# An induced-attention and gated-MLP kernel: weighted sums in column groups, full-height scores, gates and tables, and a re-searched order

## The chip, the cores and the metric

The kernel runs on one NeuronCore of a Trainium2 chip. The metric is the device time of one execution in microseconds (us); lower is better. Engines are named as in the profile: PE is TensorE (matmuls; PEld are its weight loads), ACT ScalarE, DVE VectorE, POOL GpSimd, SP SyncE, which here only starts DMAs. PSUM, where matmuls put their results, has eight banks.

## The reference

Four batches of 12,416 tokens with 128 channels, 32 inducing vectors, and an MLP with 1536 hidden units:

```python
def mab(q, kv):
    s = scale * (q @ kv.transpose(0, 2, 1))
    s = s - s.max(-1, keepdims=True)
    a = np.exp(s)
    a /= a.sum(-1, keepdims=True) + 1e-09
    return a @ kv
h = mab(I, x)                       # I: (B, 32, 128), x: (B, 12416, 128)
attn = mab(x, h)
gate = np.maximum(attn @ w_gate, 0.0)
val = attn @ w_val
out = gate * val @ w_out            # (49664, 128) float32
```

## The kernel before, in words

The kernel never forms the hidden units of a token. A token's attention output is a mix of the 32 rows of h with positive weights p. If a hidden unit's gate has one sign for all mixes, gate times value is a quadratic form in p, and the output is a sum over pairs (m, n) of p_m p_n times a table row that depends on h and the weights alone. So a batch needs these steps (b is the batch; the names in brackets are the planner's):

- **Load and transpose.** A batch has 97 tiles of 128 tokens: six groups of 16, and one tile over. They come in on POOL's queue (line 296). Each group is transposed, on PE in halves of 64 rows (turn, line 640) with a copy by DVE (line 650), or by a DMA on SP's queue (line 658) for the groups in BY_DMA.
- **First scores (s1a, s1b; line 685).** For each token the 32 scores against the inducing vectors, two groups at a time into two banks. A matmul contracts over 64 of the 128 channels, on the low or the high half of PE's rows; a low and a high one run side by side, on different banks. Then the halves change banks, which is a second step behind a wait for the first (the helper two). ACT takes the exponential (line 699).
- **h and its weights (ha, hb; lines 718 and 729).** The exponentials are moved through x as the stationary operand, again in halves of 64 tokens, into two banks: 32 matmuls for a group's h, and 8 with one moving column for the sums. DVE adds them up over the three pairs of groups (hacc, lines 743 and 745). A short chain on DVE and PE (lines 755 to 794) divides by the sums and gives hT, with one more column for the sum over the inducing vectors.
- **Gates (g1, g2; line 884) and products.** hT times the weights w_gate and w_val, in halves and two steps; DVE makes masks and scaled copies, and 16 products U of shifted copies (line 989), and a fifth, narrower set, u58.
- **Tables (T, line 1033; T5, line 1068).** The products are contracted with w_out in halves of 64 rows, four tables T of 128 rows each, two at a time in two banks, each in two steps, and T5. DVE copies them out (lines 1050, 1052, 1082).
- **Second scores (S, line 819).** hT as a stationary operand of 32 columns, four column groups of PE at once with four tiles of tokens; DVE copies them out (line 831).
- **Pairs (e, line 1257; f, line 1266).** A matmul with a 0/1 matrix adds up two scores for each pair, and ACT takes the exponential of 1024 columns at a time, into a ring of six buffers F: 192 times in all, 48 per batch. e5 and F5 (lines 846 and 859) do it for the fifth table; er, or and os for the tile over.
- **Outputs (o, line 1312).** For each token tile, 18 half-height matmuls of F with the tables, in two steps a and b with a wait between. DVE normalises three tile pairs at once (lines 1339 and 1344) and SP stores them (line 1356).
- **Check.** POOL and DVE test that the signs hold (lines 1117 to 1172); if a count is left at the end, a general kernel follows. It is not run here.

The first batch's loads, transposes, first scores and h have a section of their own (lines 305 to 512), which ends about 28 us into the span; its matmuls are full height. Everything behind it is a list of steps that the class Plan puts in an order. Each step has an engine, a duration, the steps it depends on, and perhaps PSUM banks that it takes or frees. Within an engine the order is written out: ORDER holds, in two digits each, the numbers of the steps of PE, ACT, DVE, POOL and SP, and BANKS a bank for a step where there is a choice. Plan.order (lines 158 to 215) goes through these queues with the durations, and by the times that it reckons it interleaves the engines' instructions into one program. So the orders within the engines were found beforehand by a search over this model, and the durations decide which bank a step gets.

Of the kernel before, what the change touches and what calls it, by code (L numbers as in the profile page):

```python
# [20 lines left out]
NU = 3  # L21
# [4 lines left out]
BEGIN = {}  # L26
BY_DMA = {(2, 3), (3, 3), (2, 1), (3, 1), (2, 5), (3, 5)}
# [4 lines left out]
        "0600041T022f5b1j1B5e0c1n0d2j5h2h5u2L5v5k081h5n2N5A5B5x1V5q5y1R1P5D5E0z5G2t5H0A0B0C2z0D0E0F"  # L32
        "0G5s1z5J2P5K0Z1x0+0Q0R1l2v0S0T5O0U0V0W1D0X2R5U1p2d1q1r1s1t1F1u1G1H1I1J3m1K2l2x2m2n2o2p2B2q"
        "2C2D3i2E2F3k2G1X1Y1Z4c1+1-232024254g2627283S3g5Y0ab339b83A2-3w30313Q32332T342U2V3y2W2X3U2Y"
        "3b1c3C3c4Q5W5+bp644s65bq3E3F4O3G3H3I4w3Jbjbkbd3o3O3p3q4M3r3s423t4344bh45464u47bmbvbn7bbw3W"
        "bsbt4y3X3Y4K3Zby3+bz4i3-4S7f4T4U4e4V4W4+4X7p4-507N51527L4A534B4C7d4D4E8J4F6r6s6t6u8D8H6v6w"
        "6x6ybD608l4k6R4l4m6S4n4o7J4p6I7H6J6K6L896MbN6N797v6O6PbL7tbJ857h8b7i7j7rgU7k7lbR7m7P8p7Q7R"
        "877S7T7x7U7y7z9c7A7B7C917X9e7Y7Z8Fh27+9o7-80628d9u8e8fgZ8r8g8h8i9s74he938n94hfbVbPbW9M8th8"
        "8uh98v988w8x8y8L9a8M8N9G8O8P9qhbhcaq8Q8Tam8U8V9K8W8X9waI8Y9x9yh69z9Ahk9I9g9Bhl9h9iaa9j9k9O"
        "9l9P9Qa89R9SaG9Thhhia4a6hnho9Wd09X9Yak9Zac9+ao9-adaedCafagbTahcgchaEcicjd4ckasdAataueSavaw"  # L40
        "aCaxcldycmcndYhsaKd2aLaMd+aNaOaSdgaPaTaUdwaVaWewaXcGdWcHdkcxcyczdicAeuhycBdecCcDcEeehAdEey"
        "dFdGegdHdIdMdJc+dNdOeadPdQe0d6dRd7d8fvd9dafzdbdme-dndodpecdqe2drfhe3e4ese5e6fjeie7ejekf-el"
        "emf3eIeneJffeKeZeLeMcVf1hEeNfdhKfVhLeAfBeBfxeCeDg9eEeFflgrfmfngtfofpgxfqeUhGeVf5gbf6f7fXf8"
        "f9fDfagdfEfFfZfGfHgffLfIfMfNiTfOfPiPfQghiVgigjgkgvglg1gmjpg2g3j9g4g5jri5i6g6jni7i8j7i9iajL"
        "ibicivj3iwiRhCgzjlgAgBjNgCgDgHgEhIgIgJkcgKgLkaiminj5ioipk6iqirisk8itj-gMiXjRiYiZkqi+i-jbj0"
        "kujcjdkUjejfjPjtjgjujvkSjwjxksjBjyjCjDkojEjFkQkwjGl4kxkylokzkAkekBl6kfkglqkhkijTkjl2jUjVl8"
        "jWjXlkkEjYkFkGkOkHkIlmkJiKm2k1k2lAmqlBlClOlDlElalFlbm4lcmoldlekWlfkXkYmkkZk+mmlsk-ltlul+lv"
        "lwm0mwlxmxmylKmzmAlQmgmBmhlMmimjmsmtlSlTlUlVlWm6lXm7m8m9mambmH"
    ),
    (  # L50
        "1U2g1k1C1o2k2i2M5w091i2O5C1W1S1Q2u5I2A5t1A2Q1y1m2w1E2e2S2y3n3j3l4d4h3T3h0b3a3B3x3R3z3V3D4R"
        "4tbr4P4xbl3P4Nbi4v7cbx4z4L4j7g4f7q7O7M7e8K8I8E8m617K7I8a7a7w7u868c7sbS8q889d929f8G9p639v8s"
        "9t8ohg9Nha999b9H9raran9LaJh79Jhmaba9aHa5a7d1alapdDbUaFd5dBeTaDdzdZd3d-dhdxexdXdldjevdfefez"
        "ehc-ebe1fwfAf0edfietfkg0f4fge+f2fefWfCfygagsgugyhHgcfYgef+ggiUiQiWgwjqjajsjoj8jMj4iSjmjOhJ"
        "kdkbj6k7k9k0jSkrkvkVjQkTktkpkRl5lpl7lrl3l9llkPlnm3mrlPm5mpmlmnl-m1lLlRlN"
    ),
    (
        "070105035c5f0e0g0k0f5i0i0h0j0m0l5l0w0s0n0p5o0v0x0t0r5z5r0y0K0u0J0o5F0I0q0L0O0H0M5L0N5M0P0-"
        "5N1e1f5P5Q5R5S5T0Y5V1v1w1L1M2r2s2H2I2122292a5Zb4b91a1b35362Z2+3d3e1d5-5X686667696a6c6b3K6d"
        "3L6jbe6B3u3v766f48496ebo6k6lbu6n6p6q6CbAbB40416m6D4Y4Z6h6o5477556g4G6i4HbC6A6z6HbE6F6EbF6G"  # L60
        "6TbG4q4rbHbIbO6QbMbKgV7n7o7V7W7D7E72h3818273g+8j8k759596bQbXbZb+b-bYc1c0c28z8Ac3c4hd8R8Scp"
        "c6ca8Z8+9C9Dc8cX9m9nce9Uc9hj9Vcrcbhpcfcca0a1cscdaic5ajcYc7cqhqhrayazcohtcuctcwcvaQaRhuaYaZ"
        "cIhvhwhxhzcFhBdKdLdSdTdcddcTdsdte8e9cUeoepcWhFeOePhPhOhMhNhQhShRhTi1eGeHhZfrfshUeWeXi3igif"
        "fbfchVhXfJfKi4fRfSh-i2gngoi0h+hWg7g8hYihidilixiehDikiigFgGijiugNgOj1j2jhjijzjAjHjIiMkCkDkk"
        "kliIjZiJj+kKkLk3iLk4lGlHlglhiNl0l1lylzmCmDmumGmvlYlZmcmdmI"
    ),
    (
        "b55a5d5g5j5m5p58b0b2bagWbfgYgRgT10b7bcg-1112131415161718191gh1h46U6V6W6X6Y6Z6+6-707178cJcK"
        "cLcMcNcOcPcQcRcScZiyiziAiBiCiDiEiFiGiHiO"
    ),  # L70
    (
        "59bb1N1O2J2c2b2Kbgb6b137383f3M3N4b4a57564I4Jh5h0gX7G7F8384gS978C8B908-9E9Fa2a3aAaBa+a-dVdU"
        "dudvereqeQeReYftfUfufTgqgpgPgQjjjkjKjJkmknkNkMk5liljlJlImEmFmemfmJ"
# [7 lines left out]
    "2-2-1-0-----1---------------------------------------2-----------------------0------------1"  # L81
    "---------------------------------1-------2-----------------1------------------------------"
    "---2-------1-----------2------------0---------------2-----------------0-------2-----------"
    "----------------------0-----------------1-------1------------2-----0--1--1--1------0-----1"
    "-----2----1-----0---2-0----------------------------0----------------2--------0------------"
    "--0------------2---------------------------------0-------------------------2--------------"
    "-2-----------------0-------0--------------------------------------------------------------"
    "----0---------------------------------1--------------------------------------1------------"
    "------0-----------0----1-----1-2-0-1-----0----------------------1----------------2--------"
    "2--------------0------------0-----------------------------------------------------------2-"  # L90
    "--------------0-----------------2-------------------0------------2---------------2--------"
    "---------2-------0-----------------0---------------1-----------------0-------0------------"
    "1----2----1--------0-----------2----------1---0-1-----0----------------------2------------"
    "-------------0--------------0------------1---------------------------------2-------1------"
    "----------------------------------1-----------------0-------0-----------------0-----------"
    "----0-------------------------------------------1-------------------------1---------------"
    "1----------2--"
# [4 lines left out]
class Op:  # L102
    __slots__ = (
        "name", "eng", "dur", "post", "deps", "emit", "take", "frees", "goal", "dma", "near",
# [4 lines left out]
class Plan:  # L109
# [3 lines left out]
    BANKS = {"E": 2, "D": 4}  # L113
    ENGINES = ("PE", "ACT", "DVE", "POOL", "SP")

# [3 lines left out]
    def op(self, name, eng, dur, emit, deps=(), post=None, take=None, frees=(), goal=1e9, dma=0.0):  # L119
        o = Op()  # L120
        o.name, o.eng, o.dur, o.emit, o.take, o.goal, o.dma = name, eng, dur, emit, take, goal, dma
        o.post = {"PE": 0.21, "ACT": 0.15, "DVE": 0.07, "POOL": 0.1, "SP": 0.1}[eng] if post is None else post
        o.frees = [f for f in frees if f]
# [34 lines left out]
    def order(self, begin, sequences, near=()):  # L158
# [12 lines left out]
        done = []  # L171
        while len(done) < len(ops):
            best = None
            for e in self.ENGINES:
# [50 lines left out]
def quadratic_body(ctx, tc, x, inducing, moe_w_gate, moe_w_val, moe_w_out, out):  # L225
# [39 lines left out]
    ones16 = keep([P, P], FP16, "ones16")  # L265
    indT = keep([P, M], FP16, "indT")
# [38 lines left out]
    def first_batch(sp, psum):  # L305
# [33 lines left out]
        dve.memset(ones16, 1.0)  # L339
        warm = st([P, BLK], FP16, "warm", 1)  # L340
# [262 lines left out]
    def two(step, n, mm, o, prev):  # L603

        if step:
            after(*prev.tail)
        for i in range(n):
            ya = mm(0, step, i)
            yb = mm(1, 1 - step, i)
        o.tail = (ya, yb)  # L610
        return o.tail

# [3 lines left out]
    def prepare(b):  # L616
        s = state[b]
        s["turn"], s["load"] = {}, {}
        for q in (NQ, *range(NQ)):
# [13 lines left out]
            if q < NQ and (b, q) not in BY_DMA:  # L633
                o = op(f"turn{b}.{q}", "PE", 0.55, None, [load, *(war or [])], take=("D", 2))
# [20 lines left out]
            else:  # L655
# [10 lines left out]
        o = op(f"s1r{b}", "PE", 0.25, None, [s["turn"][NQ]], take=("E", 1))  # L666
# [4 lines left out]
                out=p1r[:, 0:M], in_=ebanks(o)[:, 0, 0:M], func=AF.Exp, scale=sm_scale  # L671
# [991 lines left out]
```

## Time and profile before

| | |
|---|---|
| median of 3 runs | 299.63 us (299.54 to 303.91) |
| profiled execution | 300.5 us, of which 298.5 us span |
| instructions in the span | 15,634 |
| PE busy, granted clock (mean) | 255.7 us, 0.94 |
| ACT busy | 215.0 us |
| DVE busy | 186.8 us |
| first matmul behind the first batch's section | 28.72 us |
| first output matmul (line 1312) | 72.04 us |
| last output matmul issued, end of the span | about 289, 298.5 us |

The profile is a page for one execution with busy times by engine, forty slices of the span, DMA queues, and groups of instructions; the trace behind it can be asked for the waits of an engine (who waited for whom), for instructions in order of time, and for busy times and counts of instructions in any stretch. A releaser "issue" means that the engine waited for nothing that the profile shows. Times of matmuls include the pipeline behind them, so the price of a matmul in a row of equal ones is read from the difference of start times, not from its length.

### The profile page before, as it was taken

What the parts mean: (1) busy time and instruction counts of PE and PEld (TensorE: products, weight loads), DVE (VectorE), ACT (ScalarE), POOL (GpSimd) and SP (SyncE); (2) the same over time, 40 slices, a digit from 0 to 9 for tenths busy, and PEclk for the clock granted to TensorE, in tenths of its full rate; (3) what the DMA queues carried; (4) which work ended last, traced back from release to release, by engine and by line L of the source; (5) the groups of instructions that cost most, each with busy time, mean ns of one, the idle gap of its engine ahead of it and who ended that gap; (6) DMA issues with size and microseconds to landing.
All of it is one profiled execution on the core that took longest, in us unless ns stands there. A gap on an engine that the chain in (4) does not pass through costs nothing.

```text
span 298.5 us, 15634 instructions
## 1 busy us (share of the span) xinstructions
PE 255.7 (86%) x7251; PEld 201.6 (68%) x7251; DVE 186.8 (63%) x383; ACT 215.0 (72%) x248; POOL 84.6 (28%) x146
## 2 busy tenths in 40 slices
PE   7497776787889784999998987999999999999970
PEld 3386444775666673885876775876877878887850
DVE  3656967366567672787576473785578794565560
ACT  4173757355479653879898875998999999999910
POOL 3594200149600310019502000079030004921200
PEclk9689976589999997999999997999999999999996
DMA  7989996659949736228950440341352250355343
GB/s 279 417 227 200 215 212 123 109 99 202 188 196 179 193 118 134 110 111 151 171 210 21 172 155 2 120 168 40 125 199 113 96 231 4 127 196 224 136 185 116
DMA packets 30039, 46.83 MB, mean 157 GB/s; under 512 B 16624, under 2 KB 17296, under 8 KB 29968
## 3 DMA queue, kind: packets, MB, share of 16 engines
q1 hardware_dynamic: 25056, 35.04, 35.6%
q0 software_dynamic: 4864, 10.72, 19.8%
q8 instruction: 58, 0.95, 1.4%
q14 instruction: 13, 0.11, 0.1%
q10 hardware_dynamic: 48, 0.02, 0.0%
HBM read 27.80 MB, written 25.43 MB: 178 GB/s over the span
## 4 chain that ended last, share of the span: by engine, by line


## 5 line engine op out<-in xcount | busy, mean ns | idle before, releaser
L1266 ACT ACTIVATE F<-AL 128x1024 f16<-128x1024 f32 x192 | 184.1, 1030 | 45.2 <-PE AL L1257 43.8
L1312 PE MATMUL AL<-T,F 64*128 64x129 f16 x3456 | 134.7, 219 | 5.4 <-issue 3.6
L1312 PEld LDWEIGHTS <-F 64*128 64x128 f16 x3456 | 108.0, 95 | 32.5 <-PE AL L1312 18.6
L1257 PE MATMUL AL<-S,pairs 64*128 64x512 f16 x384 | 75.0, 387 | 2.0 <-ACT F L1266 1.2
L1344 DVE TENSOR_TENSOR osb<-AL,rzo 128x768 f32<-128x768 f32 x64 | 61.2, 956 | 2.7 <-DMA out_dram<-osb 0.8
L1117 POOL TENSOR_TENSOR far<-S 128x768 f16<-128x768 f16 x16 | 23.4, 1467 | 84.4 <-DVE U L989 83.8
L1339 DVE RECIPROCAL rzo<-AL 128x6 f32<-128x6 f32 x64 | 12.5, 196 | 47.7 <-PE AL L1312 47.1
L1033 PE MATMUL AL<-wo,U 64*128 64x128 f16 x768 | 29.1, 227 | 1.0 <-issue 1.0
L1033 PEld LDWEIGHTS <-U 64*128 64x128 f16 x768 | 25.3, 100 | 5.1 <-issue 2.0
L1257 PEld LDWEIGHTS <-pairs 64*128 64x128 f16 x384 | 22.1, 95 | 6.1 <-issue 4.7
L1117 POOL TENSOR_TENSOR far<-far 128x768 f16<-128x768 f16 (+2 forms) x20 | 25.0, 1249 | 1.6
L296 POOL DMA_DIRECT2D x<-in_x_dram x18 | 9.7, 553 | 40.1 <-PE AL L729 19.0
L650 DVE COPY xT<-AL 128x2048 f16<-128x2048 f16 x12 | 14.6, 1220 | 6.3 <-PE AL L640 6.1
L831 DVE CAST S<-AL 128x1024 f16<-128x1024 f32 x12 | 14.3, 1214 | 2.6 <-PE AL L819 2.5
L1157 POOL TENSOR_SCALAR eps<-eps 128x1 f32<-128x1 f32 x4 | 0.8, 189 | 49.2 <-DVE eps L1142 49.2
L718 PE MATMUL AL<-p,x 64*128 64x32 f16 x576 | 10.8, 176 | 3.9 <-issue 3.8
L685 PE MATMUL AL<-indT,xT 64*128 64x32 f16 x576 | 10.8, 175 | 3.6 <-DMA xT<-x 1.4
L685 PEld LDWEIGHTS <-xT 64*128 64x128 f16 x576 | 9.7, 94 | 5.5 <-issue 3.0
L718 PEld LDWEIGHTS <-x 64*128 64x128 f16 x576 | 9.9, 95 | 5.3 <-issue 4.7
L427 DVE COPY xT<-xT_ps 128x1024 f16<-128x1024 f16 (+1 forms) x15 | 8.5, 582 | 6.8 <-PE xT_ps L426 6.7
L447 ACT ACTIVATE p1a<-s_ps 128x256 f16<-128x256 f32 (+2 forms) x16 | 5.2, 332 | 10.1 <-PE s_ps L445 9.9
L699 ACT ACTIVATE p<-AL 128x1024 f16<-128x1024 f32 x9 | 9.2, 1021 | 3.2 <-PE AL L685 3.2
(157 smaller groups left out, 270.9 us busy)
## 6 DMA issues: line engine op xcount, KB each, us to landing
out_dram<-osb SPq DMA_DIRECT2D x64, 384.0 KB, 3.3
x<-in_x_dram POOLq DMA_DIRECT2D x18, 512.0 KB, 11.2
x<-in_x_dram SPq DMA_DIRECT2D x9, 512.0 KB, 6.5
x<-in_x_dram SPq DMA_DIRECT2D x6, 256.0 KB, 7.9
wg<-in_moe_w_gate_dram POOLq DMA_DIRECT2D x1, 384.0 KB, 4.8
wv<-in_moe_w_val_dram POOLq DMA_DIRECT2D x1, 384.0 KB, 7.1
wo<-in_moe_w_out_dram POOLq DMA_DIRECT2D x1, 384.0 KB, 8.4
out_dram<-osr SPq DMA_DIRECT2D x4, 64.0 KB, 2.3
```

Source lines behind the costliest of these rows:

```text
L296: pool.dma_start(out=x16(b, t0, n), in_=xv[b][:, t0 : t0 + n, :])
L650: dve.tensor_copy(out=xTs[q].rearrange("p t (h j) -> p h t j", h=2), in_=ps)
L685: return pe.matmul(ps[:, k, t, :], xTs[qs[k]][ROWS[half], t, :], indT[ROWS[half], :], start=step == 0 and t == 0, stop=step == 1, skip_gro ...
L718: pe.matmul(ps[:, r, 0:M], l, m, start=k == 0 and t == 0, stop=k == 1, skip_group_check=True,)
L831: dve.tensor_copy(out=S[b % 2][:, gs[0] : gs[0] + 2, :], in_=dbanks(o))
L1033: pe.matmul(ps[:, k, 0:P], U[js[k] % NU][r, i, t].rearrange("p k m -> p (k m)"), wo[r, t, :], start=(step, i, t) == (0, 0, 0), stop=(step, ...
L1117: pool.tensor_tensor(out=dst, in0=in0, in1=in1, op=f)
L1257: pe.matmul(ebanks(o)[:, r, :], pairs[ROWS[r], par, j, :], S[b % 2][ROWS[r], g, :], start=True, stop=True,)
L1266: lambda o=o, j=j: act.activation(out=dst[:, j], in_=ebanks(o), func=AF.Exp, scale=sm_scale,),
L1312: pe.matmul(ps[:, k_, :], l, m_, start=step == 0 and j == 0, stop=step == 1 and j == n - 1,)
L1339: lambda: dve.reciprocal(out=rzo[rr], in_=view()[:, :, :, P : P + 1]),
L1344: lambda: dve.tensor_tensor(out=dst[:, :, 3 * h6 : 3 * h6 + 3, :], in0=view()[:, :, :, 0:P], in1=rzo[rr].broadcast_to([P, 2, 3, P]), op=AL ...
```

## The change

Four things change together.

- First scores, gates, tables and T5 use all 128 rows in one matmul, and no second step. The helper two goes. A table takes one bank instead of two tables taking two, with its own copy.
- h and its weights: the exponentials become the stationary operand of 32 columns, and x moves (128 columns), spread over four column groups of PE by tile number; the sums are made likewise with a matrix of 1/32 (part16). One step ha replaces ha and hb; hacc is now 256 columns wide, and the sums over the four groups are made by a matmul with stackI (the step zp, which has two products now).
- The model of the search gets two terms: SWITCH, 0.1 for a change of tiling (each step has a mode: 0 for halves, 1 for full height, 2 for column groups), and Fetch, which counts PE's instructions (rec) and delays PE where a block of 256 is worked off before the next is there. Some PE durations are changed with it (S 0.65 to 0.44, turn 0.55 to 0.50, vp 0.6 to 0.4).
- ORDER and BANKS are new throughout, so the orders of all five engines are.

```diff
+FETCH = (100, 256, 3.5, 1.0)
 ORDER = (
...
 class Plan:
+    SWITCH = 0.1
+    class Fetch:
+        def __init__(self):
+            self.left, self.ahead = FETCH[0], 0.0
+        def late(self, o, server):
+            done, wait = 0, 0.0
+            while o.rec - done >= self.left:
+                done += self.left
+                t = o.start + wait + o.dur * done / o.rec
+                wait += max(0.0, self.ahead - t)
+                t = max(t, self.ahead)
+                self.ahead = t + FETCH[2] + (FETCH[3] if server > t else 0.0)
+                self.left = FETCH[1]
+            self.left -= o.rec - done
+            return wait
...
+                if e == "PE" and o.mode != mode:
+                    t += self.SWITCH
...
+            if o.eng == "PE":
+                mode = o.mode
+                o.end += fetch.late(o, server)
...
+        dve.memset(part16, 1.0 / M)
...
-    p1r = main([P, P], FP16, "p1r")
-    pool.memset(p1r, 0.0)
+    p1r = main([P, M], FP16, "p1r")
-    hacc = main([P, 2, M + 1], FP32, "hacc")
+    hacc = main([P, 2 * P], FP32, "hacc")
...
-                def mm(k, half, t):
-                    return pe.matmul(
-                        ps[:, k, t, :], xTs[qs[k]][ROWS[half], t, :], indT[ROWS[half], :],
-                        start=step == 0 and t == 0, stop=step == 1, skip_group_check=True,
-                    )
-                two(step, CT, mm, o, o1)
+                    for t in range(CT):
+                        pe.matmul(ps[:, i, t, :], xTs[q][:, t, :], indT, start=True, stop=True)
...
-            ha = op(f"ha{b}.{u}", "PE", 0.52, None, [e], take=("D", 2))
-            hb = op(f"hb{b}.{u}", "PE", 0.52, None, [ha, s["p1r"] if rest else None])
+            o = op(
+                f"ha{b}.{u}", "PE", 0.57, None, [e, s["p1r"] if rest else None], take=("D", 1),
+                mode=2, rec=80 + 4 * rest,
+            )
+            def rows(o=o, b=b, qs=qs, dst=dst, rest=rest):
+                ps = dbank(o)
+                n = 2 * CT
+                flat = dst.rearrange("p k t m -> p (k t) m")
+                for t in range(n + rest):
+                    r = t % 4
+                    l = flat[:, t, :] if t < n else p1r
+                    x_ = x16(b, qs[t // CT] * CT + t % CT if t < n else NT - 1)[:, 0, :]
+                    pe.matmul(
+                        ps[32 * r : 32 * r + 32, 0:P], l, x_, start=t < 4,
+                        stop=t >= n - 4 + (rest and r == 0),
+                    )
+                for i in range(2):
+                    for r in range(4):
+                        t = 8 * r + 4 * i
+                        pe.matmul(
+                            ps[32 * r : 32 * r + 32, P : 2 * P], part16,
+                            flat[:, t : t + 4, :].rearrange("p t m -> p (t m)"),
+                            start=i == 0, stop=i == 1 and not (rest and r == 0),
+                        )
...
+            pe.matmul(dbank(o)[:, 0:M], hacc[:, 0:P], stackI[:, 0, :], start=True, stop=True)
+            pe.matmul(dbank(o)[:, M : 2 * M], ones32, small["zs"], start=True, stop=True)
...
+            for k, w in enumerate((wg, wv)):
+                for t in range(NFF):
+                    pe.matmul(
+                        ps[:, k, t, :], w[:, t * P : (t + 1) * P], hT, start=True, stop=True
+                    )
...
+                    def mmT(i=i, j=j, first=chain[0]):
+                        for t in range(NFF):
+                            pe.matmul(
+                                dbank(first)[:, 0:P], U[j % NU][:, i, t].rearrange("p k m -> p (k m)"),
+                                wo[:, t, :], start=(i, t) == (0, 0), stop=(i, t) == (1, NFF - 1),
+                            )
```

More of the change, by code (lines that the diff above doesn't have):

```diff
@@ L37 @@
[L37 to L41, printed above, removed]
@@ L718, in rows @@
                         pe.matmul(
-                            ps[:, r, 0:M], l, m, start=k == 0 and t == 0, stop=k == 1,
-                            skip_group_check=True,
-                        )
-                for t in range(0, CT + (rest and k), 4):
-                    for r in range(2):
-                        if t < CT:
-                            l = dst[ROWS[r], k, t : t + 4, :].rearrange("p t m -> p (t m)")
-                        else:
-                            l = p1r[ROWS[r], :]
-                        pe.matmul(
-                            ps[:, r, M : M + 1], l, ones16[ROWS[r], 0:1], start=False, stop=k == 1,
-                            skip_group_check=True,
-                        )
@@ L734, in prepare @@
-            ha.emit = lambda o=ha, f=rows: f(0, o)
-            hb.emit = lambda o=hb, f=rows: f(1, o)
-            for q, o in zip(qs, (ha, hb)):
+                            ps[32 * r : 32 * r + 32, P : 2 * P], part16,
+                            flat[:, t : t + 4, :].rearrange("p t m -> p (t m)"),
+                            start=i == 0, stop=i == 1 and not (rest and r == 0),
+                        )
+                if rest:
+                    pe.matmul(ps[0:M, P : P + M], part16, p1r, start=False, stop=True)
@@ L767, in prepare, with joined @@
         )
-        o = s["zp"] = op(f"zp{b}", "PE", 0.5, None, [zs], take=("D", 1))
-        o.emit = lambda o=o: pe.matmul(dbank(o)[:, 0:M], ones32, small["zs"], start=True, stop=True)
+        o = s["zp"] = op(
+            f"zp{b}", "PE", 0.5, None, [zs, s["h"]], take=("D", 1), mode=1, rec=8
+        )
+        def joined(o=o):
+            pe.matmul(dbank(o)[:, 0:M], hacc[:, 0:P], stackI[:, 0, :], start=True, stop=True)
+            pe.matmul(dbank(o)[:, M : 2 * M], ones32, small["zs"], start=True, stop=True)
@@ L1061, in tables @@
-        o1_ = op(f"T5a{b}", "PE", 0.4, None, [a3], take=("D", 2))
-        o2_ = op(f"T5b{b}", "PE", 0.4, None, [(o1_, 0.2)])
-        def mm5(step, o):
-            ps = dbanks(o1_)
-            def mm(k, half, t):
-                return pe.matmul(
-                    ps[:, k, 0:64], u58[ROWS[half], t].rearrange("p i m -> p (i m)"),
-                    wo[ROWS[half], t, 64 * k : 64 * k + 64], start=step == 0 and t == 0,
-                    stop=step == 1 and t == NFF - 1,
-                )
-            two(step, NFF, mm, o, o1_)
@@ new lines, in tables, with mm5 @@
+                s["T"].append(
+                    op(f"Tc{b}.{j}", "DVE", 0.27, table_out, [chain[1], *T_prev], frees=[chain[0]])
+                )
+        o = op(f"T5{b}", "PE", 0.69, None, [a3], take=("D", 1), mode=1, rec=24)
+        def mm5(o=o):
+            for t in range(NFF):
+                pe.matmul(
+                    dbank(o)[:, 0:P], u58[:, t].rearrange("p i m -> p (i m)"), wo[:, t, :],
+                    start=t == 0, stop=t == NFF - 1,
+                )
+        o.emit = mm5
```

310 lines of the change are left out of this document (134 added, 176 removed).

## The prediction

> **What bounds the kernel now.** I read the page first: TensorE (PE) is busy for 86% of the span, ScalarE (ACT) for 72%, and PE has holes only in the first 190 us. The third row is the granted clock in tenths, by slices of 7.5 us.
>
> ```profile
> span 298.5 us, 15634 instructions
> PE 255.7 (86%) x7251; PEld 201.6 (68%) x7251; DVE 186.8 (63%) x383; ACT 215.0 (72%) x248; POOL 84.6 (28%) x146
> PEclk9689976589999997999999997999999999999996
> q8 instruction: 58, 0.95, 1.4%
> ```
>
> Then the waits of PE and of ACT (us in total, times, longest). ACT's 43.8 us say that it starves for scores that PE makes, so PE leads. Of PE's own waits, six rows have the releaser "issue": PE waited for no semaphore. The first two and the last of the six stand here; with 3.6, 1.8 and 1.0 between them they add up to 17.3 us. The longest true dependency after the first batch is the 2.2 us for hT.
>
> ```profile
> PE AL L729 <- issue: 6.2, 2, 3.8
> PE AL L718 <- issue: 3.8, 3, 2.6
> ...
> PE AL L819 <- DVE hT L794: 2.2, 2, 1.7
> ...
> PE AL L685 <- issue: 0.9, 1, 0.9
> ...
> ACT F L1266 <- PE AL L1257: 43.8, 42, 4.7
> ```
>
> What are the issue waits? I cut the span at the ends of these waits and counted instructions. Each row is a stretch: its length, then matmuls and weight loads with their counts, DVE, ACT, POOL, and the granted clock.
>
> ```profile
> 46.91:52.84 5.93, 3.29 (x128) 2.65 (x129) 4.10 (x9) 3.64 (x4) 0.00 (x0) 0.56 0.40 79
> 52.84:56.56 3.72, 2.79 (x128) 2.50 (x128) 2.03 (x4) 1.02 (x1) 1.06 (x2) 0.50 0.34 39
> 56.56:62.48 5.92, 5.80 (x128) 5.19 (x128) 1.31 (x3) 2.55 (x4) 0.00 (x0) 0.60 0.79 158
> 62.48:65.94 3.46, 2.47 (x128) 2.02 (x128) 2.37 (x7) 2.74 (x3) 2.41 (x4) 1.00 0.47 60
> 110.45:116.37 5.92, 2.08 (x128) 1.87 (x128) 1.16 (x3) 1.94 (x2) 0.53 (x1) 0.96 1.04 208
> 116.37:120.14 3.77, 3.76 (x126) 3.20 (x128) 2.10 (x5) 2.05 (x2) 0.00 (x0) 0.61 0.15 30
> 169.22:172.95 3.73, 3.23 (x128) 2.79 (x129) 1.65 (x4) 2.26 (x4) 0.00 (x0) 1.00 0.55 211
> 256.00:260.56 4.56, 4.56 (x134) 3.89 (x130) 2.31 (x4) 4.45 (x6) 4.33 (x4) 1.00 0.46 176
> ```
>
> Between issue waits lie 128 matmuls and 128 weight loads, 256 instructions, again and again. The instruction queue moved 58 packets; 7251 + 7251 instructions are 56.6 times 256. So PE gets its instructions in blocks of 256, and a block that is worked off in less time than the next takes to come (3.5 to 3.7 us in three of the rows, 5.9 us where the other DMA traffic is heavy) leaves PE dry: 2.47 us of work in a stretch of 3.46, 2.08 in 5.92. The last row is a block of the ordinary mix, 4.56 us of work, and no wait. Short matmuls are therefore dear here by their number. The second cost stands in the clock column: after the waits PE ran at half clock (0.56, 0.50, 0.60, 0.61). Its busy time times the missing share of the clock is 3.29 x 0.44 + 2.79 x 0.5 + 5.80 x 0.4 + 3.76 x 0.39 = 6.6 us; the slices of the page that begin at 37 and 179 us, both at 0.7, with some 1 us each by the same reckoning, make it 8.5.
>
> [...]
>
> **The change part by part.** Full-height forms first. In the built order the pairs of 64-row matmuls become single matmuls over 128 rows: first scores 576 to 288, gates 192 to 96, tables 768 to 384, the fifth table 192 to 48. The column sums (582 + 150) become 291 + 75. In all about 1270 matmuls and as many weight loads go, 2550 of 14,500 instructions, ten blocks of 57. The prices are differences of start times in these rows (start, length, matmuls); the last four are from the first batch and are full height already.
>
> ```profile
> 62.97 0.55 PE L718 MATMUL AL<-p,x 64*128 64x32 f16 x32
> 63.37 0.18 PE L718 MATMUL AL<-p1r,x16r 64*128 64x32 f16 x2
> 63.40 0.24 PE L729 MATMUL AL<-ones,p 64*128 64x1 f16 x8
> 63.50 0.16 PE L729 MATMUL AL<-ones,p1r 64*128 64x1 f16 x2
> ...
> 130.24 0.41 PE L769 MATMUL AL<-zs,ones 128*128 128x32 f32 x2
> 130.59 1.04 PE L846 MATMUL AL<-S,pairs 64*128 64x512 f16 x8
> ...
> 135.97 0.51 PE L1033 MATMUL AL<-wo,U 64*128 64x128 f16 x12
> 136.41 0.62 PE L819 MATMUL AL<-xT,hT 128*32 128x512 f16 x8
> 136.96 0.51 PE L1033 MATMUL AL<-wo,U 64*128 64x128 f16 x12
> 137.31 0.59 PE L1257 MATMUL AL<-S,pairs 64*128 64x512 f16 x4
> 137.74 0.83 PE L1033 MATMUL AL<-wo,U 64*128 64x128 f16 x24
> ...
> 96.40 0.21 PE L819 MATMUL AL<-xTr,hT 128*32 128x128 f16 x1
> 96.64 0.57 PE L685 MATMUL AL<-indT,xT 64*128 64x32 f16 x32
> 97.04 0.17 PE L884 MATMUL AL<-hT,wg 64*128 64x33 f16 x1
> ...
> 24.70 0.38 PE L426 MATMUL xT_ps<-eye,x 128*128 128x128 f16 x4
> 24.92 0.26 PE L466 MATMUL z_ps<-p1a,ones 128*128 128x32 f16 x4
> ...
> 25.61 0.35 PE L469 MATMUL hT_ps<-p1a,x 128*128 128x32 f16 x8
> 25.81 0.25 PE L466 MATMUL z_ps<-p1a,ones 128*128 128x32 f16 x4
> ```
>
> First scores: 32 half-height matmuls take 97.04 - 96.64 = 0.40 us; 16 full ones at (25.81 - 25.61)/8 = 25 ns take 0.40. Tables: 12 half ones take 137.31 - 136.96 = 0.35 us, 24 do the work of 12 full ones, which at (24.92 - 24.70)/4 = 55 ns take 0.66; 36 such groups save 1 us. Gates are like the scores. What these parts save is instructions. Scores, gates and tables also lose the wait between their two steps; other work stood between the steps, so I cost it at nothing.
>
> [...]
>
> h and its weights in column groups: one tile now takes 32 + 8 half-height matmuls, (63.37 - 62.97) + (63.50 - 63.40) = 0.50 us, two such groups per unit, three units per batch, three batches: 9 x 1.0, and the odd tile. After: 40 matmuls with 32 stationary columns and 128 moving ones, four column groups at once. No row has this form. The nearest is the second scores, the same 128*32 tile: 8 matmuls of 512 columns in 136.96 - 136.41 = 0.55 us. The pair scores run two at once, and two rounds of 512 columns take 137.74 - 137.31 = 0.43; so the eight run four at once, the other 0.12 is the change of tiling after them, and 128 columns cost 0.43/32 = 13 ns: 0.53 us for 40. The other end is no overlap at all: 40 x 55 ns = 2.2 us. I take 0.55, near the row of the same tile, so 9 x 0.45 = 4 us saved; the ends reach from 4.2 saved to 11 lost.
>
> Changes of tiling: a table piece right before the second scores takes 136.41 - 135.97 = 0.44 us instead of 0.35, so entering another form costs 0.09, and leaving it the 0.12. The built order has 47 such changes before and 99 after: 52 x 0.1 = 5.2 us more. The joined product for h and z is one 32-column float matmul more per batch; the old one took 130.59 - 130.24 = 0.35, 0.25 without its change of tiling: 0.75 for three. PE work: -4 - 1 + 0.75 + 5.2 = +1 us.
>
> The fetch waits: I wrote each PE step of the new order down with these prices and cut the list every 256 instructions. In the old order twelve blocks, all before 190 us, hold only 1.9 to 3.0 us. In the new one the shortest four hold 3.3, 3.8, 3.9 and 3.9 us, all others 4.06 and more. Against 3.5 to 3.7 us nearly nothing is left; against 5.9 us, where x is loading (up to about 53 us), two blocks still wait some 1.5 each. I keep 3 us: -14.3. Without waits the clock stays up: -8.5, no cover needed.
>
> What lies beside: the accumulation on DVE now takes 256 columns where it took 66, 0.22 us to about 0.42 (bounds: those two rows below), x9, 1.8 us on an engine with 63%; two table copies become four half as wide. All hidden, but for 0.2 us per batch on the way to hT. SP now has two transposes of batch 2 before the first stores instead of one; the ring of three store buffers covers six groups of outputs. If that cover went, DVE and then PE would wait for one transpose, 6.1 us (last row below). The loads of batch 3 pass two of POOL's squares, long before they are used. One DVE memset more at the start lies under the loads.
>
> ```profile
> L745 DVE TENSOR_TENSOR hacc<-hacc,AL 128x66 f32<-128x66 f32 x6 | 1.3, 223 | 11.3 <-PE AL L729 11.3
> ...
> L1050 DVE CAST T<-AL 128x256 f16<-128x256 f32 x4 | 1.7, 421 | 4.4 <-PE AL L1033 4.4
> ...
> xT<-x SPq DMA_TRANSPOSE x6, 6.1
> ```
>
> The sum, against the profiled run of 300.5 us (span 298.5, 2.0 around it): 300.5 + 1 - 14.3 - 8.5 = 278.7, and 0.9 off to stand to the median of 299.6: 277.8. I say 278.
>
> **Rivals.** 1. The gain in the first stage is hidden. Outputs cannot begin before DVE has made its products and PE the tables; in the old run they begin at 72.04.
>
> ```profile
> 30.00:40.00 10.00, 7.20 (x254) 4.50 (x247) 9.02 (x14) 7.98 (x9) 2.13 (x5) 1.00 1.07 215
> ...
> 72.04 0.46 PE L1312 MATMUL AL<-T,F 64*128 64x129 f16 x10
> ```
>
> The stretches above up to 65.94 hold 2.64 + 0.93 + 0.12 + 0.99 = 4.7 us of waits and 5.2 us of lost clock. If DVE keeps all of it, 9.9 us stay: 288. For it: DVE is busy for 9.02 of the 10 us from 30. Against: it is for 2.03 of 3.72 and 1.31 of 5.92 us in the stretches from 52.84.
> [...]
> 3. The issue waits do not depend on the number of instructions: 300.5 + 1 - 0.9 = 301, no change. For it: the block of 256.00 has none of these waits at the same count. Against: the waits recur at multiples of 256. [...]
> 4. Slower: the column groups do not overlap. A single 128-column matmul of that tile took 96.64 - 96.40 = 0.24 us, 0.12 without the change of tiling; 40 of these are 4.8 us instead of 1.0, x9 = 38 us: 278 + 38 = 316. It decides from about 75 ns for a matmul (9 x 40 x (75 - 13) ns = 22 us). For it: the small moving size, a weight load for each. Against: the second scores overlap fully.
>
> **How the numbers follow.** Forecast 0.70, rival 1 0.08, rival 2 0.08, rival 3 0.07, rival 4 0.07. The likeliest gives 278, on its own 268 to 285: 268 if the 3 us of waits left and the 2.2 for hT go too and the new order packs PE's steps closer by 5, a guess that no row gives; 285 if the waits left are double and half the clock's loss stays (3 + 4). Rivals 1 and 2 at 288 and 289 bring the range to 290. A change under 2%, 294 to 306, cannot be told from none here. Faster: 0.70 + 0.07 + 0.07 = 0.84. Same: rival 3 and the rest of 1 and 2, 0.09. Slower: 0.07.
>
> **What would show it.** Right: about 47 instruction packets; issue waits of PE of 3 us or less; no clock under 0.9 after 60 us; the 40 matmuls of a unit within 0.6 us; outputs beginning near 60 us instead of 72; ACT's wait for scores down to about 25 us. Wrong: issue waits of the same sum at fewer packets, column matmuls far more than 13 ns apart, or full-height ones at 80 ns.

## The result and the profile after

The changed kernel takes 281.29 us in the median of four runs (279.67 to 286.95), the kernel before 300.43 on the same chip; the ratio is 0.9325 with a 95% interval of 0.9206 to 0.9444. The forecast was 278 us, 268 to 290, faster with 0.84. A second set of four runs gave 279.59 us (278.95 to 280.10) and a ratio of 0.9269 (0.92 to 0.9337). The first set's profile is of its slowest run, in which the DMA engines moved only 22 to 52 GB/s from 74 to 78 us, so the profile shown here is of the second set: 280.1 us, of which 278.2 are span.

The page's rows first, the same ones as of before:

```profile
span 278.2 us, 13101 instructions
PE 248.8 (89%) x5979; PEld 192.2 (69%) x5979; DVE 186.9 (67%) x389; ACT 214.0 (77%) x248; POOL 84.2 (30%) x145
PEclk9779999998999999999999999999999999999996
q8 instruction: 48, 0.79, 1.2%
```

The clock's row has one slice under 9 between the first batch and the end, an 8; before, there were 7, 6, 5 and 8 in a row and two more 7s. 48 packets of instructions came instead of 58. Then the waits of PE and of ACT (us, times, longest):

```profile
PE AL L1302 <- issue: 2.0, 2, 1.6
PE AL L838 <- DVE hT L813: 1.9, 2, 1.7
...
PE AL L1034 <- issue: 1.0, 1, 1.0
PE AL L703 <- issue: 0.7, 1, 0.7
...
ACT F L1254 <- PE AL L1245: 21.9, 31, 3.3
```

Three rows with the releaser "issue" are left, 3.7 us against 17.3, and ACT starves for 21.9 us instead of 43.8. All four issue waits stand at PE's instruction number 187 of a block of 256, counted from the first: the thirteen of before stood at 188, but for one at 191. The trace also has the packets of the instruction queue (q8), 16,384 bytes each: each of the four waits ends 1.4 to 1.5 us after such a packet was moved, and each of the thirteen of before 1.2 to 1.6 us after one. So what PE waits for is seen, and not only reckoned from the count. Stretches between such points (length, PE, PEld, DVE, ACT, POOL, clock, DMA share, GB/s):

```profile
47.89:53.81 5.92, 5.78 (x128) 4.41 (x128) 4.36 (x10) 4.17 (x5) 1.06 (x2) 1.00 1.09 211
53.81:59.79 5.98, 5.91 (x127) 4.99 (x128) 5.03 (x16) 3.01 (x5) 3.42 (x3) 1.00 1.04 208
69.08:73.01 3.93, 3.93 (x129) 3.38 (x131) 2.04 (x4) 2.96 (x4) 2.34 (x5) 1.00 1.21 188
135.90:141.55 5.65, 4.99 (x129) 3.78 (x129) 3.51 (x4) 3.66 (x4) 0.00 (x0) 1.00 1.09 274
```

A block in the stage that makes the tables now holds 5.8 to 5.9 us of work at full clock; before, the four stretches from 46.91 to 65.94 us held 3.29, 2.79, 5.80 and 2.47 us, the first three of them at a clock of 0.50 to 0.60. Where other DMA traffic is heavy (the last row, 274 GB/s) a block can still come late, there by 0.66 us. Last, the steps themselves, in order of time:

```profile
45.15 0.63 PE L734 MATMUL AL<-x,p 128*32 128x128 f16 x32
45.59 0.30 PE L741 MATMUL AL<-p,part 128*32 128x128 f16 x8
45.83 0.64 PE L655 MATMUL AL<-eye,x 64*128 64x64 f16 x32
...
48.91 1.51 PE L1034 MATMUL AL<-wo,U 128*128 128x128 f16 x24
50.36 0.83 PE L1245 MATMUL AL<-S,pairs 64*128 64x512 f16 x4
...
59.02 0.93 PE L1302 MATMUL AL<-T,F 64*128 64x129 f16 x18
```

The 40 matmuls of a unit of h take 45.83 - 45.15 = 0.68 us, with a change of tiling in it, so about 0.58; the first 32 follow each other at 0.44/32 = 13.8 ns. Twenty-four table matmuls take 1.45 us with the change behind them: 56 ns each. Outputs begin at 59.02 us.

To see where the time went I split the part from the first matmul behind the first batch's section to the last output (28.7 to 289.3 us before, 28.8 to 268.7 after). Lost clock is PE's busy time at half clock times one half; the rest is what is left over, PE's work at full clock with gaps under 0.2 us.

| us | before | changed | difference | forecast |
|---|---|---|---|---|
| the part | 260.5 | 239.9 | -20.6 | -21.8 |
| issue waits | 17.3 | 3.7 | -13.6 | -14.3 |
| lost clock | 9.7 | 1.5 | -8.2 | -8.5 |
| other waits over 0.2 us | 7.1 | 7.5 | +0.4 | 0 |
| the rest: work | 226.5 | 227.2 | +0.7 | +1 |

### The profile page after: what moved, and what is told of

It is laid out like the page before. It is cut to its first block, busy times and chain, and to the rows that moved or that the text cites. A ratio compares the mean times of both kernels' runs of the same rounds, so it can differ in the third digit from the quotient of the medians.

```text
span 285.2 us, 13101 instructions
## 1 busy us (share of the span) xinstructions
PE 250.0 (88%) x5979; PEld 193.6 (68%) x5979; DVE 186.8 (66%) x389; ACT 214.1 (75%) x248; POOL 84.4 (30%) x145
## 4 chain that ended last, share of the span: by engine, by line
PE 76%; DVE 8%; ACT 6%; issue 5%; DMA 2%; POOL 0%; SPq 0%; POOLq 0%; DVEq 0%; ACTq 0%
PE AL L1302 36%; PE AL L1245 14%; PE AL L1034 8%; ACT F L1254 4%; DVE osb L1334 3%; PE AL L703 2%; PE xT_ps L452 2%; PE AL L865 2%; PE AL L734 2%; DMA out_dram<-osb 2%; PE AL L838 1%; PE warm_ps L370 1%; PE AL L655 1%; DVE hT L813 1%; ACT F L878 1%
## 5 line engine op out<-in xcount | busy, mean ns | idle before, releaser
L1245 PE MATMUL AL<-S,pairs 64*128 64x512 f16 x384 | 73.9, 380 | 2.4 <-ACT F L1254 1.2
L1034 PE MATMUL AL<-wo,U 128*128 128x128 f16 x384 | 25.4, 219 | 1.7 <-issue 1.7
L1034 PEld LDWEIGHTS <-U 128*128 128x128 f16 x384 | 21.8, 98 | 5.5 <-issue 3.9
L462 POOL CAST x<-x 128x512 f16<-128x512 f32 (+2 forms) x15 | 8.6, 575 | 8.9 <-DMA x<-in_x_dram 8.9
L703 PEld LDWEIGHTS <-xT 128*128 128x128 f16 x288 | 8.2, 96 | 2.9 <-issue 2.6
L703 PE MATMUL AL<-indT,xT 128*128 128x32 f16 x288 | 8.9, 176 | 1.3 <-issue 0.7
L452 PE MATMUL xT_ps<-eye,x 128*128 128x128 f16 x96 | 9.5, 249 | 0.2
```

Of the source, the lines that this page charges most:

```text
L452: pe.transpose(ps[:, t - t0, :], x16(0, t)[:, 0, :], eye16)
L703: pe.matmul(ps[:, i, t, :], xTs[q][:, t, :], indT, start=True, stop=True)
L1034: pe.matmul(dbank(first)[:, 0:P], U[j % NU][:, i, t].rearrange("p k m -> p (k m)"), wo[:, t, :], start=(i, t) == (0, 0), stop=(i, t) == (1 ...
L1245: pe.matmul(ebanks(o)[:, r, :], pairs[ROWS[r], par, j, :], S[b % 2][ROWS[r], g, :], start=True, stop=True,)
```

## The experiments

Theory A is the prediction's: PE gets its instructions in blocks of 256, so short matmuls are dear by their number. Against it stands theory B, rival 3 of the prediction: the waits do not hang on the number. Where an expectation gives its letters another meaning, it says so itself.

**The changed kernel again.** No edit; the profile above.

> The changed kernel as it is, for a second profile. Its first profile (285.2 us span) has one issue wait of 5.8 us at 78 us, just while the DMA engines hardly move anything, and half clock after it. Theory A (instruction blocks come late where other DMA traffic holds them up): the median stays at 280 to 282, and a profile of about 278 us span has issue waits of 5 us or less in all and less lost clock. Theory B (the wait at 78 us belongs to the order and comes every time): a wait of 5 us at the same place again.

Its theory A holds and its theory B falls: issue waits are 3.7 us in all, and the one at 78 us is 0.47 us instead of 5.8. The median, 279.59 us, lies just under the 280 to 282 expected.

**The new forms in the old order.** The changed kernel's code with the ORDER of the kernel before, carried over step by step by name, but for a division on DVE that moved; 142 changes of tiling instead of 99.

> The changed steps (full height, column groups) in the order of the kernel before, step by step, with the division moved right behind the product that it frees on DVE. 142 changes of tiling instead of 99, so 4.3 us more of PE work than after the change; the blocks of 256 hold 3.4 us or more. Theory A (the forms carry the gain, by fewer instructions): 284 to 290. Theory D (the re-searched order carries it): 294 to 300.

It took 286.59 us, ratio 0.9513 (0.9443 to 0.9583), inside A's range. On the same chip the changed kernel had 279.59. So, in the old order, the forms carry 4.9 of the 7.3%, some 15 us, and the new order adds 7 us. Split as above, issue waits are 7.0 us, lost clock 3.1 and the work 231.8, 5.3 more than before. The prediction's prices give 95 x 0.1 - 4 - 1 + 0.75 = 5.3 for that. Against this run the new order has 3.3 less of waits, 1.6 less of lost clock, and 4.6 less work for 43 fewer changes of tiling. One long wait leads here:

```profile
PE AL L1287 <- issue: 5.0, 3, 4.2
...
PE AL L719 <- issue: 1.6, 2, 1.3
```

**Each half of the change alone, in the old order.** The kernel before with the h part of the changed kernel; and with the full-height scores, gates and tables, but the old h.

> Kernel before, in its own order, with h and its weights in column groups alone: 366 matmuls and as many weight loads fewer, 65 changes of tiling instead of 47. Theory A (PE waits because blocks of 256 instructions come at most every 3.5 us, so the number of instructions counts): by the same reckoning of blocks as in the prediction the work goes from 211.6 to 209.9 us behind the first batch and the waits from 17 to 10.5; with 2 to 4 us of half clock less that is 289 to 292 us against 300.5, and PE's issue waits sum to 8 to 12 us. Theory B (the issue waits don't hang on the number): only the 1.7 us of work, 298 to 299 us, issue waits still 15 to 18 us.

> Kernel before, in its own order, with first scores, gates and tables over all 128 rows alone: 912 matmuls and as many weight loads fewer, 126 changes of tiling instead of 47. Theory A: work plus 7.7 us (79 changes of tiling at 0.1, tables 1 less), waits from 17 to 9, half clock 3 to 5 us less: 294 to 298 us against 300.5, issue waits of 7 to 11 us. Theory B: only the work, 307 to 309 us, issue waits of 15 to 18. If changes of tiling cost nothing in this place, 7 less by each.

h alone: 293.18 us, ratio 0.9738 (0.969 to 0.9786). The time is nearer to A's 289 to 292 than to B's 298, but the waits are not: 15.0 us, inside B's range of 15 to 18 and far from A's 8 to 12. What went is the lost clock, 9.7 to 3.1; the work rose by 0.3 where the expectation had 1.7 less. Full height alone: 298.24 us, 0.9914 (0.9882 to 0.9945), at the upper end of A's range. Its profile, of a run of 303.06 us, has 12.8 us of waits, 10.9 of lost clock and 5.6 more work. So B's 307 to 309 falls, but A's reckoning, at 3.6 us for every block, puts the waits too low in both runs. With h alone 11.3 of the 15.0 us end before 83 us, while x and its transpose are loading; in the stretches below a block took 4.8 to 7.0 us to come beside loads, 3.5 to 4.0 without. The two halves save 2.6 and 0.9%, both together 4.9%. That thinning one dense stretch only helps until the next block in it is late would explain this; no run tries it by itself.

**Scores and gates in halves again, in the new order.** 384 matmuls more, in the place where they were full height.

```diff
-                    for t in range(CT):
-                        pe.matmul(ps[:, i, t, :], xTs[q][:, t, :], indT, start=True, stop=True)
...
+                two(step, CT, mm, o, o1)
...
+            for step in range(2):
+                two(step, NFF, lambda k, half, t: mm(k, half, t, step), o1, o1)
```

> Changed kernel in its own order, with first scores and gates in halves and two steps again, as in the kernel before: 384 matmuls and as many weight loads more at the same PE time for the work, 12 changes of tiling fewer, so 1.2 us less work. Theory A: 16 blocks under 4 us instead of five, waits 4 us more (from 3.7 to about 8), and 1 to 3 us of half clock: 283 to 286 us against 279.6 of the changed kernel. Theory B: 278 to 280 us, issue waits still 3 to 4.

It took 286.29 us (284.36 to 288.72), ratio 0.9477 (0.9428 to 0.9525), against 279.59 with 0.9269. Issue waits are 8.1 us, as A had it (about 8), and B's 278 to 280 falls. Their main rows:

```profile
PE AL L710 <- issue: 4.6, 4, 1.4
...
PE AL L1049 <- issue: 1.2, 1, 1.2
PE AL L1193 <- issue: 1.2, 1, 1.2
...
PE AL L665 <- issue: 0.9, 1, 0.9
```

But the time is over A's range by a little, because the work rose by 2.6 us where I had 1.2 less. In six of the nine units the matmuls on both sides of the step's wait start 232 to 241 ns apart: with nothing between the two steps, each wait costs about 0.2 us, some 2 us for these six and the four gates. The rest of the 3.8 stays open. Lost clock rose by only 0.2 us, where A had 1 to 3.

**Empty instructions.** One empty instruction behind each full-height and column matmul of the change (three behind those of T5), and twice as many.

```diff
+    def pad(n):
+        for _ in range(n):
+            pe.nop(hint="pad", nofuse=True)
...
+                        pad(2)
```

> The changed kernel with 2550 empty instructions on PE, spread behind the matmuls of scores, sums, gates and tables: as many instructions as before the change, with the array work of after. Theory A (a block of 256 instructions takes 3.5 us and more to come, so their number is what cost the time): the cuts of the list at every 256 then hold 1.6 to 3.5 us in some 20 places, 16 us of waits at 3.6 us for a block and 24 us at 4.0, and clock lost after them: 297 to 306 us. Theory B (the gain came from the order or the shorter sums, the number of instructions is hidden): 281 to 285, with no more issue waits than in the changed kernel.

> Half of the empty instructions, one behind each matmul instead of two. Theory A: 6 us of waits at 3.6 us for a block and 10 at 4.0: 286 to 292, well under half of what 2550 cost, since a wait begins only where a block holds less work than it takes to come. Theory C (an empty instruction costs PE a fixed time of its own): half of the loss of 2550. Theory B: 281 to 283.

With two behind each matmul it took 447.78 us, with one 351.68 us. Theories A and B missed by far, and the test says little of the count; theory C, a fixed time for each empty instruction, comes near, with 72 us lost for half of them against 168. The first scores of a unit, with one and with two empty instructions behind each matmul:

```profile
48.17 3.08 PE L707 MATMUL AL<-indT,xT 128*128 128x32 f16 x32
51.19 0.61 PE L1255 MATMUL AL<-S,pairs 64*128 64x512 f16 x2
```

```profile
52.33 5.27 PE L707 MATMUL AL<-indT,xT 128*128 128x32 f16 x32
57.57 0.61 PE L1255 MATMUL AL<-S,pairs 64*128 64x512 f16 x2
```

3.02/32 = 94 ns and 5.24/32 = 164 ns for a matmul that takes 25: an empty instruction costs PE 70 ns of its own. Both rows lie at half clock, but at full clock later in these traces the steps are 91 and 162 ns just so. 2550 of them are 178 us, near the 168 measured. One thing can be read: with 58 packets of instructions as before, the heavier run has no issue wait over 0.32 us (its 44 short ones stand between the matmuls of T5, with six empty instructions each); the lighter has two, of 1.34 and 1.59 us. So the number alone makes no wait; it is the number per time.

**Stretches that need nothing.** Behind the last product of the changed kernel I put matmuls on constant operands into free PSUM, with 16 loads beside the first stretch (768 KB each by the row of DMA issues; the expectation names half of that). All of it comes on top of the computation, and it ran once.

```diff
+    half(1024)
+    full(512, 128)
+    half(1024)
+    full(512, 32)
+    column(512)
...
+    for i in range(32):
+        full(8, 128)
+        half(8)
```

> Changed kernel, and behind its last product stretches of matmuls that need nothing, in PSUM that is free: 1024 half-height ones of 32 columns, 512 full-height ones of 128 columns, 1024 half-height ones again, 512 full-height ones of 32 columns, 512 in column groups (128 columns); then 256 full and 256 half, and the same number changing form after each 8; the same with 256 column ones. Sixteen loads of 384 KB begin at about 276 us and lie beside the first stretch. Theory A (blocks of 256 instructions, 3.5 to 3.7 us each): the second half-height stretch takes 28 to 30 us instead of 19 at 18.6 ns, with a wait of 1.1 to 1.3 us at every 256th instruction; the first is longer where the loads run (4 to 6 us a block); 512 full ones of 128 columns take 28 us without waits; 512 of 32 columns 14.4 instead of 12.8; the column ones 14.4 instead of 6.8. Theory B: none of these waits, 19, 28, 19, 12.8 and 6.8 us. Changes of tiling at 0.1 us: the mixed stretches are 63 x 0.1 = 6.3 us longer than the sum of their two parts.

```profile
276.00:290.00 14.00, 5.12 (x357) 4.91 (x358) 0.00 (x0) 0.00 (x0) 0.00 (x0) 0.50 0.86 306
357.82:361.55 3.73, 1.89 (x128) 1.78 (x128) 0.00 (x0) 0.00 (x0) 0.00 (x0) 0.50 0.02 4
```

These two rows, with the columns of the stretches above, show where the loads run: a DMA share of 0.86 with 306 GB/s in the first stretch, 0.02 in the second. The half-height stretches (line 1414) fall into groups of 128 matmuls and their 128 weight loads, with an issue wait ahead of each. Two groups beside the loads, three without:

```profile
276.82 1.89 PE L1414 MATMUL AL<-indT,wg 64*128 64x32 f16 x128 [1.58 <-issue]
283.01 1.89 PE L1414 MATMUL AL<-indT,wg 64*128 64x32 f16 x128 [4.31 <-issue]
...
357.82 1.89 PE L1414 MATMUL AL<-indT,wg 64*128 64x32 f16 x128 [1.84 <-issue]
361.55 1.89 PE L1414 MATMUL AL<-indT,wg 64*128 64x32 f16 x128 [1.84 <-issue]
365.31 1.89 PE L1414 MATMUL AL<-indT,wg 64*128 64x32 f16 x128 [1.87 <-issue]
...
393.91 1.97 PE L1428 MATMUL AL<-eye,indT 128*32 128x128 f16 x128 [1.67 <-issue]
397.93 1.97 PE L1428 MATMUL AL<-eye,indT 128*32 128x128 f16 x128 [2.05 <-issue]
```

Without other traffic a block takes 3.5 to 3.8 us in the half-height stretch (361.55 - 357.82 = 3.73) and 3.5 to 4.0 in the column one, for 1.9 to 2.0 us of work (14.8 ns a half-height matmul, where the expectation had 18.6); beside the loads 4.8 to 7.0 (283.01 - 276.82 = 6.19), where it had 4 to 6. Here too every wait ends 1.2 to 1.6 us after a packet of the instruction queue. The packet itself takes 0.9 to 1.3 us with and without the loads. But the next one begins 1.1 to 1.5 us after PE has gone on in the second half-height stretch, and 2.4 to 4.6 us after it beside the loads: what the loads put off is the packet's start. The second half-height stretch took 27.6 us, the column one 14.9: A had 28 to 30 and 14.4, B 19 and 6.8. The 512 full-height matmuls of 128 columns ran in one piece of 30.9 us, 28.5 without the half clock at their start, with no wait. Those of 32 columns took 14.3 us, but 128 of them at 27 ns are 3.5 us, as long as a block takes to come, so they decide nothing.

The same kernel prices the changes of tiling:

```profile
447.65 0.27 PE L1414 MATMUL AL<-indT,wg 64*128 64x32 f16 x8
447.85 0.62 PE L1421 MATMUL AL<-eye,wg 128*128 128x128 f16 x8
448.40 0.27 PE L1414 MATMUL AL<-indT,wg 64*128 64x32 f16 x8
...
494.89 0.29 PE L1428 MATMUL AL<-eye,indT 128*32 128x128 f16 x8
495.12 0.62 PE L1421 MATMUL AL<-eye,wg 128*128 128x128 f16 x8
```

Eight full-height matmuls to the next form take 448.40 - 447.85 = 0.55 us, 0.445 without a change at 55.6 ns each: 0.105. Eight column ones at 13.8 ns are 0.11 of the 0.23 us: 0.12. Eight half-height ones at 13 to 15 ns are 0.10 to 0.12 of the 0.20: 0.08 to 0.10. The whole mixed stretch with column groups takes 25.0 us, its two parts without waits 14.4 + 3.5: 7.1 us for 63 changes, 0.11 each, where the expectation had 6.3.

**hT without its copy.** The wait for hT (1.7 us from 60.4) and the only half clock of the stretch, 3.4 us from 61.7, are the largest thing left. The chain for hT on VectorE, then POOL beside it, in the changed kernel:

```profile
59.39 0.19 DVE L797 TENSOR_TENSOR h<-AL,rz 128x32 f32<-128x32 f32 x1
59.62 0.19 DVE L805 TENSOR_REDUCE h<-h 128x1 f32<-128x32 f32 x1
59.84 2.22 DVE L813 CAST hT<-h 128x33 f16<-128x33 f32 x1
```

```profile
60.35 1.65 POOL L1105 TENSOR_TENSOR far<-far 128x768 f16<-128x768 f16 x1
62.08 1.47 POOL L1105 TENSOR_TENSOR far<-S 128x768 f16<-128x768 f16 x1
```

A copy of 33 columns takes 2.22 us, where its fastest of the three takes 0.19, and ends at 62.06 when POOL's squaring does, at 62.00. I took it out, first by writing h straight into hT, then with two products:

```diff
-                out=small["h"][:, 0:M], in0=dbank(o)[:, 0:M], in1=small["rz"], op=ALU.mult
...
+            for to in (small["h"], hTs[b % 2]):
+                dve.tensor_tensor(
+                    out=to[:, 0:M], in0=dbank(o)[:, 0:M], in1=small["rz"], op=ALU.mult
+                )
...
-                lambda: dve.tensor_copy(out=hTs[b % 2], in_=small["h"]), [c, *war],
```

> Changed kernel with hT written in half precision by the product of h and by its sum themselves, so that the copy from float to half (128x33, one source and target in SBUF) goes. That copy took 2.22 us once and 1.27 and 0.19 the other times, and in the slowest it ended when a squaring on POOL ended. [...] Theory D (VectorE stands still there for a reason of its own, such as its instructions coming late): the next instruction of the chain becomes the long one, 279 to 280.

> Changed kernel, hT again without the copy from float to half: the product of h is made twice from PSUM, once in float and once in half, and the sum of the float one is written to hT; the values are those of the changed kernel. In the run with hT written straight that chain had no instruction over 0.2 us and PE's waits for hT were gone. [...] Theory E (the wait is passed on: PE works earlier and meets more issue waits and the same pace of ACT later): 278.5 to 280.5 us, with PE's issue waits over 5 us instead of 3.7. The earlier run speaks for E: PE's 5563rd instruction came 1.1 us earlier than in the changed kernel, its 11,958th 0.6 us later.

In the first of the two, the sum over rounded values makes the kernel's sign test leave a count, so the general kernel follows from 269 us on, 2406.55 us in all; only the part before that is read. The second, with the sum over the float values, took 280.15 us (278.87 to 286.36), ratio 0.9292 (0.9245 to 0.9339), against 0.9269: no gain that can be told. Its chain:

```profile
59.15 0.19 DVE L798 TENSOR_TENSOR h<-AL,rz 128x32 f32<-128x32 f32 x1
59.26 0.18 DVE L798 TENSOR_TENSOR hT<-AL,rz 128x32 f16<-128x32 f32 x1
59.38 0.19 DVE L807 TENSOR_REDUCE hT<-h 128x1 f16<-128x32 f32 x1
```

The long instruction is gone and no other became long, so theory D falls. That the copy waited for POOL is argued from ends that coincide: the next batch's copy, of 1.27 us, ends at 123.80 and an instruction of POOL at 123.75, and the third, with nothing on POOL beside it, took 0.19. But the first began at 59.84, before POOL's squaring did, so how it waited stays open. Theory E holds for the time of the run profiled. PE's 2000th instruction comes 2.0 us earlier than in the changed kernel, the 3000th 0.6; issue waits are 5.8 us instead of 3.7. Then this:

```profile
135.04 0.62 PE L1303 MATMUL AL<-T,F 64*128 64x129 f16 x15 [1.87 <-issue]
...
137.49 2.00 PE L866 MATMUL AL<-S,pairs 64*128 64x512 f16 x8
```

The wait at that block is 1.87 us instead of 1.57, 3.4 us of half clock follow it (the eight matmuls behind take 2.00 us, 1.07 in the changed kernel), and the lead is used up. In the run with hT straight that wait was 1.59, the clock stayed up, and PE was still 1.2 us ahead at the last output. The expectation's last words, that its 11,958th instruction came 0.6 us later, misread the trace: it comes 1.2 us earlier. So the wait taken away is worth some 1.2 us or nothing, by what happens at one later block.

## Why the prediction was right, and where it was not

- **What bounds the kernel.** Right, and shown: the stretches reproduce a wait at every 256th instruction with nothing else to wait for, each ending 1.2 to 1.6 us after a packet of instructions, at the supply read from the old trace (3.5 to 3.7 us; measured 3.5 to 4.0), and under loads 5.9 lies inside 4.8 to 7.0.
- **The fetch waits, -14.3.** -13.6 measured. That it is the count that carries it, the run with halves shows: 8.1 us of waits against 3.7. The 3 us that I kept were 3.7, and that this is so near is luck. The prediction put them at two blocks up to 53 us; only 1.04 stands there. Waits of 1.57 and 0.66 end at 135.90 and 141.55 us, beside a later batch's loads, where it allowed none and where the blocks held 4.6 and 5.0 us of work. The 1.04 and the 1.57 stand behind these two stretches of full DMA (1.07 and 1.04):

```profile
42.63:46.85 4.22, 3.65 (x141) 2.87 (x134) 3.28 (x8) 3.97 (x5) 0.76 (x2) 1.00 1.07 214
129.64:134.32 4.68, 4.62 (x137) 3.59 (x134) 2.92 (x6) 4.63 (x6) 0.00 (x0) 1.00 1.04 254
```

For single parts in the old order the same reckoning failed: 15.0 us for h alone where it gave 10.5, 12.8 for full height alone where it gave 9.
- **Lost clock, -8.5 without cover.** -8.2, in part by luck: before, 9.7 us were lost, since the two slices at 0.7 held 1.7 and 1.5 us and not 1 each, and 1.5 us stay; the two misses nearly cancel. "No clock under 0.9 after 60 us" was wrong by one dip at 61.7 us, and that began within the 1.7 us wait for hT, not at a block.
- **h in column groups, -4.** 0.58 us a unit instead of 0.55, so 9 x 0.42 = 3.8 less. Rival 4 falls: 13.8 ns a matmul, far from 75. (Its 38 us is reckoned against 0.55 us a unit; against the 1.0 that it names it would be 34.)
- **Tables, -1; full height at 55 and 25 ns.** 56 ns and 25 ns. Rival 2 falls: its 289 us in the range, and the 80 ns, stand for 25 ns more for the load of each of 432 table matmuls, which no run shows; with a new load each, the table matmuls took 56 ns.
- **Changes of tiling, +5.2.** 0.08 to 0.12 each. The new forms in the old order, with 95 more, came to the 5.3 us of the sum.
- **Scores and gates at nothing.** This held for the change: in the old order other work stood between the steps, and the new forms in it match the sum without this term. It does not hold as a price of the form: in an order with nothing between two halves, the form with two steps costs some 0.2 us for each wait, and 2.6 us of work in all.
- **DVE beside it.** The accumulation takes 420 ns as bounded (0.42). Rival 1 falls: outputs begin at 59.02 us, not near 70.

```profile
L759 DVE TENSOR_TENSOR hacc<-hacc,AL 128x256 f32<-128x256 f32 x6 | 2.5, 420 | 1.9 <-PE AL L747 1.0 <-PE AL L741 0.9
```

- **SP's two transposes ahead of the stores.** Hidden in the run shown. In the first run, of 286.95 us, the block due at 78 us came 5.76 us late while the second transpose and a load stood unfinished to 81 us, and the packet of instructions began at 81.39; whether their order does it was not tried.
- **Rival 3.** Falls. A block's end shows no wait in the stretch of 512 full-height matmuls of 55.6 ns; in the stretches of matmuls of 13.8 to 14.8 ns without loads, waits of up to 2.05 us stand there.

## What to carry to other kernels

When PE waits for nothing that the profile shows, count its instructions between the waits; if the count repeats, add up the work of each block and compare it with the time a block takes to come, quiet and under loads. Here the forms with fewer, larger matmuls, in their new order, paid twice, by 13.6 us of waits and by 8.2 us of lost clock, with 0.7 us more of PE's own work. With the 1.7 us wait for hT taken away, one run had 5.8 us of issue waits instead of 3.7, and 3.4 us of half clock behind a later block, so a gain is read at the last output and not where the wait was.

## What the runs showed of the hardware

- An empty instruction on PE cost 70 ns, more than a full-height matmul of 128 columns (56 ns) with its weight load.
- Beside 16 loads of 768 KB a block of 256 PE instructions took 4.8 to 7.0 us to come instead of 3.5 to 4.0, and what came later was the start of its packet, not the packet's own time.
- A copy of 33 columns on VectorE from float to half, both in SBUF, took up to 2.22 us beside GpSimd's work instead of 0.19; the same values written from PSUM took 0.18. The two slow copies ended within 0.06 us of an instruction of POOL; whether and how they waited for it, no run here shows.
- The length of an issue wait alone does not say whether the clock falls. Waits of 1.57 and 1.59 us left it up, and one of 1.87 us at the same place was followed by 3.4 us of half clock, which cost some 1.2. But with h alone a wait of 3.07 us, to 57.67 us, left it up, and with halves in the new order one of 1.33 us, to 47.14 us, was followed by half clock. In the traces of the kernel before and of the changed kernel's first run, stretches of half clock between the first batch and the end last 3.41, 6.83 or 13.65 us. What decides whether a wait is followed by one, no run shows.
